# Two value units of a decode attention kernel, each loaded by two queues

## The chip, the core and the metric

The kernel runs on one core of one Trainium2 chip. The engines that matter here are TensorE (PE), VectorE (DVE), ScalarE (ACT) and SyncE (SP). SyncE and ScalarE can both issue loads from the chip's memory into the on-chip memory of 128 partitions; each has a queue of its own in the profile (q1 is SyncE's, q10 ScalarE's), and the packets of both are moved by the core's 16 DMA engines. The metric is the device time of one execution in microseconds, as the median of the runs.

## The reference

One token is decoded against a long cache. `x` has 448 values; there are 16 query heads in 8 groups of two that share a key and value head, 65536 cached positions and a head size of 256. Everything large is bf16. Cut to what matters:

```python
xn = layernorm(x)
q = (xn @ wq).reshape(1, 1, 16, 256)              # 16 query heads
scores = einsum(q, k_cache) * 256 ** -0.5         # k_cache: 8 x 65536 x 256, each head for two queries
o = softmax(scores) @ v_cache                     # v_cache: 8 x 65536 x 256
attn = o.reshape(1, 1, 4096) @ wo                 # 4096 x 448
r = xn @ w_r                                      # a router over one token: it is always chosen
y = (silu(xn @ w_gate) * (xn @ w_up)) @ w_down * sigmoid(r)
out = x + attn + xn + y
```

The two caches are 512 MB (2 x 8 x 65536 x 256 x 2 bytes); wq, wo and the three feed-forward matrices are some 12 MB more. Each byte is used once.

## The kernel before

**Units and slots.** Each head's 65536 positions are spread over the 128 partitions, 512 consecutive positions in each. The kernel cuts a head into four units of 128 positions in each partition. A unit is thus 128 stretches of 64 KB, one to a partition, 8 MB in all. Keys make 32 units and values 32. The tensor `ring` holds three slots of one unit each: slots 0 and 1 take keys, slot 2 takes values. A slot is a semaphore too (`slot0` to `slot2`): a load adds 16 to it when it is complete, and PE waits for the count that the unit it needs will bring it to.

**Order of loads.** The list of loads is written out by hand and issued by SyncE in that order: `item` puts the waits that a load needs, and then the load, on SyncE's program. The waits are on PE having done with what stood in the slot: `FREE, u` is the end of PE's transposes of key unit u, `VFREE, t` the end of its products with value unit t. Keys run one head ahead of values, so that the softmax's maximum of a head is known when its values are used.

**The end.** The last head's values are the units NT to NT + 3 (28 to 31). There are no keys left by then, so the key slots take values too. SyncE's list ends like this, where `slot_item(kind, unit, slot, parts, waits)` loads one unit:

```python
slot_item("v", NT, 0, None, [("FREE", NU - 2)])
item("wg", ...); item("wd", ...); item("wo", ...)     # into slot 2, after VFREE NT - 1
slot_item("v", NT + 1, 1, None, [("FREE", NU - 1)])
slot_item("v", NT + 2, 0, None, [("VFREE", NT)])
slot_item("v", NT + 3, 1, ...two parts..., [("VFREE", NT + 1)])
# then the last rows of wo, in five small loads
```

"The second and third units" of the change are NT + 1 and NT + 2. NT + 3 goes into the slot of NT + 1, so it is issued only when PE has used NT + 1.

On PE, `ending` puts its work in this order: the maximum of the last head, `values(NT)`, the feed-forward (`pe_ffn1`, `pe_ffn_hT`, `pe_ffn2`), the output product of the first seven heads (`pe_attn`), `values(NT + 1)`, `values(NT + 2)`, `values(NT + 3)`, and the output product of the last head. `values(t)` is 64 matmuls into `ps_o`, in two chunks (`pe_V`), each after ScalarE has copied the softmax weights of its positions (`p_sb`, by `act_pc`).

ScalarE has two small loads of its own there: `hop` writes the outputs of the first seven heads to memory (`o_flat`) and reads them back in another layout (`oT_h`). All loads of the program show as one line of the source in the profile, L892.

Of the kernel before, what the change touches and what calls it, by code (L numbers as in the profile page):

```python
# [21 lines left out]
def bass_parallel_sum__gqa_block_cached__moe_arch_mod__decode_kernel(  # L22
# [20 lines left out]
    P = 128  # L43
    _, Hkv, Sk, Dh = A_k_cache.shape
# [16 lines left out]
    SBN = HC * CH  # L61
    SETS = SBN // SETN
    U = NPP // SBN
    NT = U * (Hkv - 1)
    NU = U * Hkv
# [27 lines left out]
    slots = [ring[:, i * SLOT:(i + 1) * SLOT] for i in range(NSLOT)]  # L93
# [98 lines left out]
    prog = {e: [] for e in engines}  # L192
    here = [("S", 0)]
# [7 lines left out]
    def put(e, kind, key, fn, sem):  # L201
        if ghost[0] and e == "pe":
            prog[e].append(("g" + kind, lab(e), key, fn, sem))
        elif not ghost[0]:
            prog[e].append((kind, lab(e), key, fn, sem))

    def W(e, *key):
        put(e, "w", key, None, None)
# [3 lines left out]
    def O(e, key, fn, sem=None, n=1):  # L212
        key = key if isinstance(key, tuple) else (key,)
        if not ghost[0]:
            weight[key] = n
        put(e, "o", key, fn, sem or e)
# [17 lines left out]
    items = {}  # L234
    semtot = {}
    fed = {}

    def item(key, parts, need=()):
        for n in need:
            W("sp", *n)  # L240
        for ap, src, sem in parts:
            semtot[sem] = semtot.get(sem, 0) + 16
            items[key] = (sem, semtot[sem])
            prog["sp"].append(("d", here[0], ("DMA", key, len(prog["sp"])), (ap, src), sem))

    def rows_src(kd, u, o, J):
        src = A_k_cache if kd == "k" else A_v_cache
        n0 = (u % U) * SBN + o
        return src[0, u // U].rearrange("(p n) d -> p n d", p=P)[:, n0:n0 + J, :]

    def slot_item(kd, u, s, parts=None, need=()):

        o = 0
        for k, (sem, J) in enumerate(parts or [("slot%d" % s, SBN)]):
            ap = slots[s][:, o * Dh:(o + J) * Dh]
            item((kd, u, k), [(ap.rearrange("p (j d) -> p j d", d=Dh), rows_src(kd, u, o, J), sem)],
                 need[k] if isinstance(need, dict) else need if k == 0 else ())
            o += J
        fed[(kd, u)] = (s, parts or [("slot%d" % s, SBN)])

    def flat_src(src, n):
        return src.rearrange("a b -> (a b)").rearrange("(p n) -> p n", p=P)

# [6 lines left out]
    def wo_rows(f0, f1):  # L270

        return A_wo[0:(Hq - rep) * Dh, :].rearrange("(p f) n -> p f n", f=FR)[:, f0:f1, :].rearrange("p f n -> p (f n)")
# [21 lines left out]
    item("wg", [(wg_area[:, 0:WGN // 2], flat_src(B_w_gate, F), "wg"), (wg_area[:, WGN // 2:WGN], flat_src(B_w_up, F), "wg")], [("VFREE", NT - 1)])  # L294
    item("wd", [(wd_area.rearrange("p (s x) -> p s x", s=2), B_w_down.rearrange("(s p t) n -> p s (t n)", s=2, p=P), "wd"), (x_again, A_x[0], "wd")])
    item("wo", [(wo_all[:, 0:(FR - WX) * D], wo_rows(0, FR - WX), "wo")])
    slot_item("v", NT + 1, 1, None, [("FREE", NU - 1)])
    slot_item("v", NT + 2, 0, None, [("VFREE", NT)])
    slot_item("v", NT + 3, 1, [("last%d" % k, J) for k, J in enumerate(LAST)], [("VFREE", NT + 1)])
    LATE_AT = [FR - sum(LATE[k:]) for k in range(len(LATE) + 1)]  # L300
    for k in range(len(LATE)):
# [107 lines left out]
    def mm(*a, **k):  # L409
        return pe.matmul(*a, **k)  # L410
# [87 lines left out]
    def k_JT(s):  # L498
        u, sl = divmod(s, SETS)
        W("pe", "EVQ", s)  # L500
        if sl == 0:
            W("pe", "SCOPY", u - 1)
        n0 = sl * SETN

        def f(it):
            for jj in range(GN):
                o = ps_sn[:, n0:n0 + SETN, :].rearrange("p (m j) i -> p m j i", j=GN)[:, :, jj, :]
                ins = mm(o, lhsT=s2[s % 2][:, jj * P:(jj + 1) * P], rhs=sel_bf[:, :, :], start=True, stop=True)
            return ins

        O("pe", ("JT", s), f, "jt")
        if sl == SETS - 1:
            dve_scopy(u)
# [14 lines left out]
    def pe_m1t(b):  # L528
        W("pe", "M1", b)
        W("pe", "OTSB", min(b - U, NT - 1))  # L530
        O("pe", ("M1T", b), lambda it: mm(ps_m[0:rep, C_BIG:C_BIG + P], lhsT=m1[:, :], rhs=ident_f[:, :],
                                          is_transpose=True, start=True, stop=True))
        W("dve", "M1T", b)
        O("dve", ("GMAX", b), lambda it: nc.vector.tensor_reduce(out=gmax[:, :], in_=ps_m[0:rep, C_BIG:C_BIG + P], axis=AX.X, op=ALU.max))
        W("dve", "GMAX", b)
        W("dve", "BC", b - 1)
        O("dve", ("DIAG", b), lambda it: nc.vector.tensor_scalar(out=diag[:, :], in0=ident_f[0:rep, 0:rep], scalar1=gmax[:, 0:1],  # L537
                                                                 scalar2=None, op0=ALU.mult))
# [25 lines left out]
    def pe_tot(t):  # L564
        W("pe", "NEGMAX", t + U - 1)
        W("pe", "PC", t, 0)

        def f(it):
            return mm(ps_m[0:P, C_TOT:C_TOT + NH * rep].rearrange("p (f i) -> p f i", f=NH), lhsT=ones_f[:, :],
                      rhs=rowsum[:, :].unsqueeze(1).to_broadcast([P, NH, rep]), start=True, stop=True)  # L570

        O("pe", ("TOT", t), f)
        W("dve", "TOT", t)
        W("dve", "OTSB", t - 1)
        O("dve", ("RS", t), lambda it: nc.vector.reciprocal(out=rs[:, :, :], in_=ps_m[0:P, C_TOT:C_TOT + NH * rep]))  # L575
# [81 lines left out]
    def hop(k, dst, src):  # L657
        items["oh", k] = ("oh%d" % k, 16)
        prog["act"].append(("d", here[0], ("DMA", "oh", k), (dst, src), "oh%d" % k))
# [116 lines left out]
    def values(t):  # L776
        for c in range(HC):
            pe_V(t, c, t == NT, t == NU - 1, True)

    def ending():  # L780
        here[0] = ("S", 1)
        T = NU - 1
        n = NU * SETS
        k_JT(n - 2)
        k_QK(n - 1)
        pe_turn()
        k_JT(n - 1)
        W("pe", "OROW")
        pe_m1t(T)
        pe_bc(T)  # L790
        W("pe", "OTSB", NT - 1)
        W("act", "DMA", ("oh", 0))
        hop(1, oT_h[:, :], o_flat.rearrange("r d -> (r d)").rearrange("(p f) -> p f", f=FR))
        values(NT)
        pe_tot(NT)
        pe_ffn1()
        pe_ffn_hT()
        pe_ffn2()
        pe_attn()
        W_item("dve", "wd")  # L800
        O("dve", "XN_AGAIN", lambda it: nc.vector.tensor_scalar(out=xn_again, in0=x_again, scalar1=stat[0:1, 7:8], scalar2=stat[0:1, 4:5],
                                                                op0=ALU.add, op1=ALU.mult))
        W("dve", "XN_AGAIN")
        W("dve", "FFN2")
        W("dve", "ATTN")
        W("dve", "SIG")
        O("dve", "YS", lambda it: nc.vector.scalar_tensor_tensor(
            out=sum_f, in0=ps_y, scalar=stat[0:1, 6:7], in1=xn_again, op0=ALU.mult, op1=ALU.add))
        W("dve", "YS")
        O("dve", "YX", lambda it: nc.vector.tensor_tensor(out=sum_f, in0=sum_f, in1=x_again, op=ALU.add))  # L810
        W("dve", "YX")
        O("dve", "SUM", lambda it: nc.vector.tensor_tensor(out=sum_f, in0=ps_a, in1=sum_f, op=ALU.add))
        values(NT + 1)
        W("pe", "SUM")
        W("pe", "SCOPY", T)

        O("pe", "FIN_BASE", lambda it: fin(sum_f, 0, ones_f[0:1, 0:1], first=True))
        values(NT + 2)
        values(NT + 3)
        dve_ob(T)  # L820
        pe_oT(T)

        def fin_x(it, k):
            for f in range(*LATE_AT[k:k + 2]):
                ins = fin(wo_all, f * D, oT_h[:, f:f + 1])
            return ins

        for k in range(len(LATE)):
            W_item("pe", ("wx", k))
            O("pe", ("FIN_X", k), lambda it, k=k: fin_x(it, k))  # L830
        W("pe", "OTSB", T)
        for k, (i, f0, f1) in enumerate(ENDS):
            W_item("pe", ("wo_end", k))

            def f(it, k=k, i=i, f0=f0, f1=f1):
                for hf in range(f0, f1):
                    ins = fin(wo_end, (i * NH + hf) * D, oT_sb[:, hf, i:i + 1], last=k == len(ENDS) - 1 and hf == f1 - 1)
                return ins

            O("pe", ("FIN", k), f)  # L840
        W("dve", "FIN", len(ENDS) - 1)
        W("act", "FIN", len(ENDS) - 1)
        O("act", ("RESULT", 1), lambda it: nc.scalar.activation(out=res_bf[:, DA:D], in_=ps_s[32:33, 0:D - DA], func=ACTF.Copy), "res")  # L843
        O("dve", ("RESULT", 0), lambda it: nc.vector.tensor_copy(out=res_bf[:, 0:DA], in_=ps_s[0:1, 0:DA]), "res")
        W("sp", "RESULT", 0)
        W("sp", "RESULT", 1)
        prog["sp"].append(("d", here[0], ("OUT", 0), (out[0], res_bf), "out"))
# [275 lines left out]
```

## Time and profile before

| what | value |
|---|---|
| median of 3 runs | 1275.57 us (1275.52 to 1275.57) |
| the profiled execution | 1275.83 us |
| its span, from the first to the last instruction | 1274.5 us |
| granted TensorE clock, mean | 0.889 |
| PE busy | 953.0 us, 75% |
| DVE busy | 570.5 us, 45% |
| ACT busy | 436.9 us, 34% |
| moved by DMA | 549.22 MB, 431 GB/s over the span |

Times in the profile are microseconds from the start of the span. A row of a timeline gives the start, the duration, the engine (a q behind its name is the engine's queue of instructions that issue DMAs), the source line, the operation, what is written and read, the count, and in brackets how long the engine sat idle before it and what ended that. PE's busy share is high because its matmuls fill the time between loads; whether it or the loads set the pace is read from what its idle time waits for. The landing time of a load is counted from its issue, so it includes the time that it stands in its queue behind earlier loads.

### The profile page before, as it was taken

Reading aid. Unit: us, or ns where it says so; the run is one execution under the profiler, and the core shown is the slowest. Engines: PE = TensorE matmul, PEld = TensorE weight load, DVE = VectorE, ACT = ScalarE, POOL = GpSimd, SP = SyncE. Lnnn points to the kernel's source line nnn. Section 1 sums busy time; section 2 is a strip of 40 time slices with the busy share of each in tenths; the row PEclk is TensorE's granted clock in tenths of the full one; section 3 lists DMA queues with packets and bytes.
Section 4 is the critical chain, followed back from the end, with each engine's and each line's share of the span. In section 5 each row is a group of like instructions: output and inputs, shape, how many; then the busy total and the mean of one; then the engine's idle time right before and its main releaser. Section 6 shows DMA issues by size and latency. Waiting matters only on the chain. (4 is left out here: it accounts for less than half of the span.)

```text
span 1274.5 us, 23469 instructions
## 1 busy us (share of the span) xinstructions
PE 953.0 (75%) x9718; PEld 625.3 (49%) x9718; DVE 570.5 (45%) x1078; ACT 436.9 (34%) x656; POOL 8.0 (1%) x38
## 2 busy tenths in 40 slices
PE   3998977678767769777778677687777688777844
PEld 3676655445544445444455454454454555444411
DVE  4665544445434455444454344453444544444310
ACT  1554533244322433324233243343333334323300
POOL 2000000000000000000000000000000000000000
PEclk9998998889888899888899888898878988888876
DMA  9999999999999999999999999999999999999998
GB/s 406 430 434 431 443 430 430 438 428 442 432 432 428 438 430 442 430 432 432 434 430 442 430 432 436 430 436 436 432 430 438 428 436 436 432 430 438 426 431 367
DMA packets 11841, 549.22 MB, mean 431 GB/s; under 512 B 1442, under 2 KB 1844, under 8 KB 2356
## 3 DMA queue, kind: packets, MB, share of 16 engines
q1 hardware_dynamic: 11652, 549.03, 99.7%
q8 instruction: 8, 0.13, 0.0%
q10 hardware_dynamic: 176, 0.02, 0.0%
q14 instruction: 5, 0.04, 0.0%
HBM read 549.04 MB, written 0.01 MB: 431 GB/s over the span
## 5 line engine op out<-in xcount | busy, mean ns | idle before, releaser
L410 PE MATMUL ps_t<-ident_f,ring 128*128 128x128 f32 x4096 | 589.2, 286 | 83.6 <-DMA ring<-in_A_k_cache_dram 62.7
L469 DVE COPY kt_all<-ps_t 128x1024 bf16<-128x1024 bf16 x768 | 487.0, 685 | 295.6 <-PE ps_q L410 291.3
L410 PEld LDWEIGHTS ps_t<-ident_f,ring 128*128 128x128 f32 x4096 | 452.7, 144 | 236.3 <-issue 134.6
L471 ACT ACTIVATE kt_all<-ps_t 128x1024 bf16<-128x1024 bf16 x256 | 262.2, 1024 | 501.7 <-PE ps_q L410 501.6
L410 PE MATMUL ps_o<-ring,p_sb 128*4 128x512 bf16 x2048 | 177.1, 508 | 213.8 <-DMA ring<-in_A_v_cache_dram 208.9
L410 PEld LDWEIGHTS ps_o<-ring,p_sb 128*4 128x4 bf16 x2048 | 53.8, 102 | 302.6 <-issue 277.9
L410 PE MATMUL ps_q<-kt_all,q_cur 128*2 128x512 bf16 x2056 | 164.7, 397 | 0.3 <-DVE kt_all L469 0.3
L493 ACT ACTIVATE s<-ps_q 98x512 bf16<-98x512 f32 x257 | 151.8, 591 | 1.3 <-PE ps_q L410 1.3
L575 DVE RECIPROCAL rs<-ps_m 128x4 f32<-128x4 f32 x29 | 5.3, 183 | 271.5 <-PE ps_m L410 271.5
L562 ACT ACTIVATE p_sb<-S_sb 128x128 bf16<-128x128 bf16 x64 | 18.9, 307 | 271.4 <-PE ps_o L410 271.2
L410 PEld LDWEIGHTS ps_s<-sel_bf,s 128*128 128x128 bf16 x1032 | 64.1, 97 | 4.5 <-ACT s L493 1.3
L613 DVE CAST ob_sb<-ps_o 100x512 bf16<-100x512 f32 x29 | 20.1, 692 | 99.0 <-PE ps_o L410 99.0
L410 PE MATMUL ps_s<-sel_bf,s 128*128 128x8 bf16 x1032 | 63.3, 167 | 1.0 <-ACT s L493 1.0
L410 PEld LDWEIGHTS ps_q<-kt_all,q_cur 128*2 128x2 bf16 x2056 | 26.4, 79 | 45.2 <-issue 45.2
L410 PEld LDWEIGHTS ps_m<-rowsum,ones_f 128*128 128x128 f32 x58 | 11.8, 255 | 21.3 <-issue 21.3
L471 ACT ACT_TABLE_LOAD x7 | 9.0, 1283 | 27.8 <-PE ps_q L410 27.8
L522 DVE TENSOR_REDUCE m1p<-S_sb (+1 forms) x33 | 13.9, 422 | 4.4
L410 PE MATMUL ps_m<-rowsum,ones_f 128*128 128x4 f32 x58 | 14.4, 318 | 0.0
L552 ACT ACTIVATE S_sb<-S_sb,negmax 128x512 bf16<-128x512 bf16 x16 | 13.2, 851 | 3.3 <-DVE negmax L546 3.3
L410 PE MATMUL ps_m<-diag,ones_f 2*128 2x2 f32 x58 | 11.2, 260 | 3.8 <-DVE diag L537 1.0
L410 PEld LDWEIGHTS ps_m<-diag,ones_f 2*128 2x128 f32 x58 | 8.7, 187 | 10.7 <-DVE diag L537 10.7
L520 DVE CAST S_sb<-ps_s 128x256 f32 (+1 forms) x33 | 13.7, 416 | 0.1
(90 smaller groups left out, 122.7 us busy)
## 6 DMA issues: line engine op xcount, KB each, us to landing
ring<-in_A_k_cache_dram SPq DMA_DIRECT2D x10, 4096.0 KB, 28.4
ring<-in_A_v_cache_dram SPq DMA_DIRECT2D x1, 6144.0 KB, 27.3
ring<-in_A_wq_dram SPq DMA_DIRECT2D x1, 3584.0 KB, 11.2
ring<-in_A_v_cache_dram SPq DMA_DIRECT2D x1, 2048.0 KB, 31.9
ring<-in_A_wo_dram SPq DMA_DIRECT2D x1, 1792.0 KB, 26.8
ring<-in_B_w_gate_dram SPq DMA_DIRECT2D x1, 1568.0 KB, 16.3
ring<-in_B_w_up_dram SPq DMA_DIRECT2D x1, 1568.0 KB, 19.6
ring<-in_B_w_down_dram SPq DMA_DIRECT2D x1, 1568.0 KB
```

Of the source, the lines that this page charges most:

```text
L410: return pe.matmul(*a, **k)
L469: O(e, ("EV", s, m), lambda it: nc.vector.tensor_copy(out=kt[:, :], in_=tb[:, :]), f"ev{m}")
L471: O(e, ("EV", s, m), lambda it: nc.scalar.activation(out=kt[:, :], in_=tb[:, :], func=ACTF.Copy), f"ev{m}")
L493: O("act", ("EVQ", s), lambda it: nc.scalar.activation(out=s2[s % 2][0:QROWS, :], in_=ps_q[0:QROWS, :], func=ACTF.Copy), "evq")
L520: O("dve", ("SCOPY", u), lambda it: nc.vector.tensor_copy(out=S_sb[:, at(it, SBN), :], in_=ps_sn), "sc")
L522: O("dve", ("SMAX", u), lambda it: nc.vector.tensor_reduce(out=m1p[:, :, at(it, 1)], in_=S_sb[:, at(it, SBN), :].rearrange("p n i -> p i n ...
L552: O("act", ("EXP", h, i), lambda it, i=i: nc.scalar.activation(out=S_sb[:, :, i], in_=S_sb[:, :, i], func=ACTF.Exp, bias=negmax[:, i:i + 1 ...
L562: O("act", ("PC", t, c), lambda it: nc.scalar.activation(out=p_sb[:, c, :, :], in_=S_sb[:, n:n + CH, :], func=ACTF.Copy), "pc")
L575: O("dve", ("RS", t), lambda it: nc.vector.reciprocal(out=rs[:, :, :], in_=ps_m[0:P, C_TOT:C_TOT + NH * rep]))
L613: O("dve", ("OB", t), lambda it: nc.vector.tensor_copy(out=ob_sb[0:OROWS, :], in_=ps_o[0:OROWS, :]))
```

## The change

Units NT + 1 and NT + 2 are each loaded in two halves by partition. SyncE issues partitions 0 to 63 at the place where it issued the whole unit, after the same waits. ScalarE issues partitions 64 to 127, after the same waits put on its own program: for NT + 1 directly behind the second `hop`, for NT + 2 behind the program part `values(NT)`. Both halves add 16 to the slot's semaphore, and PE waits for the sum. No unit, slot or wait of PE changes besides.

```diff
+    def shared_item(u, s, need):
+        ap = slots[s].rearrange("p (j d) -> p j d", d=Dh)
+        src = rows_src("v", u, 0, SBN)
+        sem = "slot%d" % s
+        item(("v", u, 0), [(ap[0:P // 2], src[0:P // 2], sem)], need)
+        other[u] = (ap[P // 2:P], src[P // 2:P], sem, need)
+        semtot[sem] += 16
+        items[("v", u, 0)] = (sem, semtot[sem])
+        fed[("v", u)] = (s, [(sem, SBN)])
+
+    def ask_other(u):
+        ap, src, sem, need = other[u]
+        for n in need:
+            W("act", *n)
+        prog["act"].append(("d", here[0], ("DMA", "other", u), (ap, src), sem))
...
-    slot_item("v", NT + 1, 1, None, [("FREE", NU - 1)])
-    slot_item("v", NT + 2, 0, None, [("VFREE", NT)])
+    shared_item(NT + 1, 1, [("FREE", NU - 1)])
+    shared_item(NT + 2, 0, [("VFREE", NT)])
...
         hop(1, oT_h[:, :], o_flat.rearrange("r d -> (r d)").rearrange("(p f) -> p f", f=FR))
+        ask_other(NT + 1)
         values(NT)
+        ask_other(NT + 2)
         pe_tot(NT)
```

On ScalarE's program the place is the end, from the write of `o_flat` to the sigmoid of the feed-forward (the two activations that write `kt_all` from `ps_t`). Before:

```order
L892 DMA o_flat<-kt_all 14x256
L552 ACTIVATE S_sb,rowsum<-S_sb,negmax 128x512 x2
L562 ACTIVATE p_sb<-S_sb 128x128 x2
L892 DMA oT_h<-o_flat 128x28
L562 ACTIVATE p_sb<-S_sb 128x128 x2
L688 ACT_TABLE_LOAD
L688 ACTIVATE kt_all<-ps_t 2x448 x2
```

And after, where the lines of the source are 19 to 21 higher:

```order
L913 DMA o_flat<-kt_all 14x256
L571 ACTIVATE S_sb,rowsum<-S_sb,negmax 128x512 x2
L581 ACTIVATE p_sb<-S_sb 128x128 x2
L913 DMA oT_h<-o_flat 128x28
L913 DMA ring<-in_A_v_cache_dram 64x32768
L581 ACTIVATE p_sb<-S_sb 128x128 x2
L913 DMA ring<-in_A_v_cache_dram 64x32768
L707 ACT_TABLE_LOAD
L707 ACTIVATE kt_all<-ps_t 2x448 x2
```

The two loads of `ring` from 64 partitions' worth of values are new: one between the hop and the weights of the next unit, one ahead of the table load.

On SyncE's program the place is the last six loads of `ring`. Before:

```order
L892 DMA ring<-in_A_x_dram 1x448
L892 DMA ring<-in_A_wo_dram 128x7168
L892 DMA ring<-in_A_v_cache_dram 128x32768 x2
L892 DMA ring<-in_A_v_cache_dram 128x24576
L892 DMA ring<-in_A_v_cache_dram 128x8192
```

And after:

```order
L913 DMA ring<-in_A_x_dram 1x448
L913 DMA ring<-in_A_wo_dram 128x7168
L913 DMA ring<-in_A_v_cache_dram 64x32768 x2
L913 DMA ring<-in_A_v_cache_dram 128x24576
L913 DMA ring<-in_A_v_cache_dram 128x8192
```

The two whole units have become two halves at the same places; what stands before and behind them is as it was.

More of the change, by code (lines that the diff above doesn't have):

```diff
@@ L259, in slot_item @@
         fed[(kd, u)] = (s, parts or [("slot%d" % s, SBN)])
+    other = {}
+    def shared_item(u, s, need):
[12 more added lines that the diff above has]
+        prog["act"].append(("d", here[0], ("DMA", "other", u), (ap, src), sem))
     def flat_src(src, n):
```

## The prediction

> **What bounds the kernel now.** I read the queue table of the page first, to see whether the loads are the limit at all.
>
> ```profile
> DMA packets 11841, 549.22 MB, mean 431 GB/s; under 512 B 1442, under 2 KB 1844, under 8 KB 2356
> q1 hardware_dynamic: 11652, 549.03, 99.7%
> q10 hardware_dynamic: 176, 0.02, 0.0%
> ```
>
> The reader is to see that one queue, q1 (SyncE's), moves all but 0.02 MB, and that its packets fill 99.7% of the 16 engines' time. q10 is ScalarE's. The kernel is a stream of 549 MB at one pace; it gets shorter only if the pace rises or a hole closes, and there is next to no hole.
>
> Second, the tail on the engine that uses the data: PE's timeline from 1218 us, where "idle before" names what it waited for.
>
> ```profile
> 1218.28 3.19 PE L410 MATMUL ps_q<-ring,oT_h 128*1 128x448 bf16 x16
> 1229.45 6.36 PE L410 MATMUL ps_o<-ring,p_sb 128*4 128x512 bf16 x64 [7.99 <-DMA ring<-in_A_v_cache_dram]
> 1248.82 5.22 PE L410 MATMUL ps_o<-ring,p_sb 128*4 128x512 bf16 x64 [12.51 <-DMA ring<-in_A_v_cache_dram]
> 1263.34 3.58 PE L410 MATMUL ps_o<-ring,p_sb 128*4 128x512 bf16 x32 [9.31 <-DMA ring<-in_A_v_cache_dram]
> 1267.41 2.74 PE L410 MATMUL ps_o<-ring,p_sb 128*4 128x512 bf16 x32 [0.48 <-PEq L1077]
> ```
>
> The four starts are the landings of units NT+1, NT+2 and the two parts of NT+3. Each wait ends with a load. The step from 1229.45 to 1248.82 is the pace: 19.37 us for one unit of 8.39 MB, which is 433 GB/s. A unit is 128 packets of 64 KB, eight for each engine, so one packet takes 19.37 / 8 = 2.42 us.
>
> Third, SyncE's queue: when each load is issued.
>
> ```profile
> 1183.18 0.34 SPq L892 DMA_DIRECT2D ring<-in_A_wo_dram  x1
> 1192.67 0.33 SPq L892 DMA_DIRECT2D ring<-in_A_v_cache_dram  x1
> 1206.05 0.33 SPq L892 DMA_DIRECT2D ring<-in_A_v_cache_dram  x1
> 1235.86 0.80 SPq L892 DMA_DIRECT2D ring<-in_A_v_cache_dram  x2
> ```
>
> NT+1 is issued 36.8 us before it lands and NT+2 42.8 us. NT+3 is issued at 1235.86, 12.96 us before NT+2 has landed. The queue never runs dry here, so a second issuer closes no gap.
>
> **The change part by part.** *Issues and waits.* ScalarE gets two more issues. Its timeline around them, before:
>
> ```profile
> 1200.16 0.51 ACT L562 ACTIVATE p_sb<-S_sb 128x128 bf16<-128x128 bf16 x2
> 1200.47 0.36 ACTq L892 DMA_DIRECT2D oT_h<-o_flat  x1
> 1204.16 0.31 ACT L562 ACTIVATE p_sb<-S_sb 128x128 bf16<-128x128 bf16 x1 [3.49 <-PE ps_o L410]
> 1206.05 0.31 ACT L562 ACTIVATE p_sb<-S_sb 128x128 bf16<-128x128 bf16 x1 [1.58 <-PE ps_o L410]
> 1206.38 1.28 ACT L688 ACT_TABLE_LOAD   x1
> 1209.09 0.96 ACT L688 ACTIVATE kt_all<-ps_t 2x448 f32<-2x448 f32 x2 [1.42 <-PE ps_t L410]
> ```
>
> The first issue comes behind the hop at 1200.47 + 0.36 = 1200.83. Its wait, FREE of the last key unit, was over when SyncE issued at 1192.67. It costs 0.36 us inside 3.49 us of idle time: zero. The second comes behind the copy of 1206.05. Its wait, VFREE of NT, is what that copy had just waited for: zero. It pushes the table load by about 0.36 us, to an end at 1208.0, and the activation behind it could not start before 1209.09: zero. Without that cover the sigmoid and the feed-forward would be 0.36 us later, which PE's 7.99 us of idle time before NT+1 takes up. SyncE issues as many loads as before, with the same waits. PE waits for the same semaphore, at a count that both halves make up; the price of that is only the later of the two halves.
>
> *When ScalarE's half can flow.* It stands in q10 behind the hop of oT_h:
>
> ```profile
> ring<-in_A_wo_dram SPq DMA_DIRECT2D x1, 1792.0 KB, 26.8
> oT_h<-o_flat ACTq DMA_DIRECT2D x1, 7.0 KB, 12.0
> ```
>
> These 7 KB need 12.0 us, though at the stream's pace they are worth 0.02 us: packets of q10 take turns with packets of q1 on each engine. The hop is through at 1200.47 + 12.0 = 1212.5, and wo, the last load ahead of NT+1 in q1, at 1183.18 + 26.8 = 1210.0. So both halves of NT+1 begin at about the same time, and neither the feed-forward's weights nor wo are pushed back by more than a packet or two. From then on each engine takes turns between a packet for the lower partitions and one for the upper, four of each for a unit, through NT+1 and NT+2: 16 packets, 38.7 us at the old pace.
>
> [...]
>
> *What a half costs.* No row of this trace has a sizeable transfer to fewer than 128 partitions, so the price has two ends. Lower end: the engines are the limit, and the pace stays at 2.42 us a packet, +0. A gain isn't in reach, since the engines' time is already 99.7% full. Upper end: the pace belongs to the ways into the partitions. Then 128 partitions take 16 packets at 2.42 us at a time, 64 take only eight, and 16 engines that all write the same half need 4.84 us a packet: +38.7 us over two units. [...] The phases of the engines are in a window of 5 us, 40 slices of 0.125 us, in which 524 is the start of one 64 KB packet:
>
> ```profile
> GB/s 0 0 0 524 0 0 0 0 1573 524 1049 0 0 524 524 1049 1573 524 524 0 0 0 0 524 0 0 0 1049 1049 1049 0 0 0 524 1049 1049 1049 1049 0 0
> DMA packets 32, 2.10 MB, mean 419 GB/s; under 512 B 0, under 2 KB 0, under 8 KB 0
> ```
>
> 32 starts are two rounds of 16. In the first round there are 1 and 6 starts up to the eleventh slice and 9 from the 14th to the 19th; the second starts with the 24th. [...] I take +28.7. I prefer the upper side to zero because the pace is one number in every stage (431 GB/s over the span, 433 here), and what the edit changes is exactly which partitions 16 engines write at once.
>
> *What follows it.* NT+1 lands about 14 us later, at 1244; PE needs 6.36 us, so NT+3 is issued near 1250. NT+2 lands at 1248.82 + 28.7 = 1277.5, so the queue still has 27 us in hand and no hole opens. NT+3 and the rest of wo go to 128 partitions as before, and the chain at the end keeps its lengths:
>
> ```profile
> 1267.41 2.77 PE ps_o L410 x32
> 1270.21 0.70 DVE ob_sb L613
> 1271.21 1.75 PE ps_s L410 x31
> 1272.98 0.36 ACT kt_all L843
> ```
>
> Sum: issues 0, waits 0, halves +28.7, tail 0. The profiled execution took 1275.83 us (span 1274.5 and 1.33 around it), 0.26 above the median of the runs. 1275.83 + 28.7 - 0.26 = 1304.3, so 1304.
>
> **The rivals.** *The halves interleave without loss.* If the engines are the limit, or an engine keeps both halves in flight so that both sides of the memory are always written, the total bytes and the pace are unchanged: NT+2 lands at 1248.8 again and the time is 1275.6. For it: every engine has one packet of each half in turn, so over two packets both halves are used evenly. [...]
>
> [...]
> [...]
>
> *A hole before NT+3.* If ScalarE's half were first served in turn with the weights, NT+1 would be complete only after everything issued before NT+2's lower half. That is 4.2 MB or 9.7 us later, at 1239; with PE's 6.36 us NT+3 is issued at 1245.5, and NT+2, ending at 1248.8 at full pace, leaves 3.3 us for the start of a transfer. If a start takes more, the stream stands still for the rest. The hop's 12.0 us include waiting, so they bound the start: a hole of at most 8.7 us, 1284, more likely 1278. Against it: the hop ahead in q10.
>
> **How the numbers follow.** Sharing with lags (+15 to +37 us): 0.46. Lockstep (over +37): 0.14. A hole, or a small loss of 3 to 15 us: 0.09. No loss: 0.27. Some gain that no row explains: 0.04. About 0.2% (2.6 us) is what a measurement of this kernel can tell from no change. So slower is 0.46 + 0.14 + 0.09 = 0.69, same 0.27, faster 0.04. The likeliest case gives 1304, its own range 1291 to 1313. The range that leaves out no more than 2 in 10 must take in the no-loss case: 1275 to 1313.
>
> **What the profile of the changed kernel would show.** q10 carries about 8.4 MB and packets of 64 KB. ScalarE's two issues stand near 1201 and 1206.4. If I am right, PE's start on NT+1 moves from 1229.45 to about 1244 and on NT+2 from 1248.82 to about 1277, NT+3 follows NT+2 by the same 14.5 us, and the DMA row stays at a full share while GB/s falls to some 250 (433 / 1.74) in between. If there is no loss, GB/s stays near 430 throughout, and the starts stay. A hole would show as a low DMA share after NT+2. [...]

## The result, and the profile after

| | before | after |
|---|---|---|
| median, us | 1275.57 (4 runs, 1275.52 to 1275.77) | 1320.14 (4 runs, 1313.7 to 1324.95) |
| ratio to before | 1 | 1.0336, 95% interval 1.0292 to 1.038 |
| profiled execution, us | 1275.83 | 1313.7 |
| its span, us | 1274.5 | 1312.4 |

The change costs 44.6 us by the medians. The profiled execution is the fastest of the four and shows 37.9 of them; the experiments come back to the rest.

The queue table of the page after:

```profile
DMA packets 11873, 549.22 MB, mean 418 GB/s; under 512 B 1474, under 2 KB 1876, under 8 KB 2388
q1 hardware_dynamic: 11524, 540.65, 96.9%
q10 hardware_dynamic: 336, 8.40, 2.8%
```

The bytes are the same, 8.4 MB of them have moved to ScalarE's queue, and the engines are as busy as they were: 96.9 and 2.8 make 99.7%. A full queue doesn't mean a full pace. That is in the windows (the last number of a row is GB/s, the one ahead of it the engines' busy share). After, from where the halves begin:

```profile
1210.00:1230.00 20.00, 6.67 (x30) 2.57 (x28) 2.37 (x6) 0.02 (x1) 0.00 (x0) 0.70 1.01 223
1230.00:1250.00 20.00, 5.37 (x16) 1.76 (x16) 1.90 (x3) 0.00 (x0) 0.00 (x0) 0.59 1.01 239
1250.00:1270.00 20.00, 3.37 (x35) 1.12 (x38) 0.00 (x0) 0.00 (x0) 0.00 (x0) 0.50 0.98 220
```

And before, in the same places:

```profile
1210.00:1230.00 20.00, 10.26 (x54) 4.17 (x56) 4.29 (x9) 0.04 (x1) 0.00 (x0) 0.78 0.98 426
1230.00:1250.00 20.00, 7.49 (x80) 2.27 (x72) 0.00 (x0) 0.62 (x2) 0.00 (x0) 0.59 1.00 432
```

With a busy share of 1.0 in both, the stream moves 220 to 239 GB/s in place of 426 to 432. PE's timeline after shows what that does to the landings:

```profile
1230.53 5.37 PE L429 MATMUL ps_q<-ring,oT_h 128*1 128x448 bf16 x16 [12.11 <-DMA ring<-in_A_wo_dram]
1266.63 6.52 PE L429 MATMUL ps_o<-ring,p_sb 128*4 128x512 bf16 x64 [30.73 <-DMA ring<-in_A_v_cache_dram]
1287.16 6.49 PE L429 MATMUL ps_o<-ring,p_sb 128*4 128x512 bf16 x64 [13.52 <-DMA ring<-in_A_v_cache_dram]
1301.34 3.58 PE L429 MATMUL ps_o<-ring,p_sb 128*4 128x512 bf16 x32 [7.69 <-DMA ring<-in_A_v_cache_dram]
1305.41 2.49 PE L429 MATMUL ps_o<-ring,p_sb 128*4 128x512 bf16 x32 [0.49 <-PEq L1098]
```

NT+1 lands at 1266.6 (before 1229.5), NT+2 at 1287.2 (1248.8), and NT+3 follows NT+2 by 14.2 us (14.5). So the 38 us of this execution arise in the two halved units and nowhere behind them. Nearly all of them, 37.2, are there when NT+1 lands. By the packets of the trace, 192 of the 256 packets of the two units have ended by then (before: 136), though NT+1 has only 128: 64 packets of NT+2's halves had ended before the last of NT+1's. NT+3 waits for PE to have used NT+1, so it is issued late too, at 1273.19 in place of 1235.86:

```profile
1273.19 5.17 SPq L913 DMA_DIRECT2D ring<-in_A_v_cache_dram  x2
```

PE also waits 12.11 us for wo, which has landed 47.2 us after its issue, not 26.8:

```profile
ring<-in_A_wo_dram SPq DMA_DIRECT2D x1, 1792.0 KB, 47.2
ring<-in_A_v_cache_dram ACTq DMA_DIRECT2D x2, 73.4
```

wo isn't on the path: PE would have waited for NT+1 anyway.

### The profile page after: what moved, and what is told of

It is laid out like the page before. It is cut to its first block, busy times and chain, and to the rows that moved or that the text cites. A ratio compares the mean times of both kernels' runs of the same rounds, so it can differ in the third digit from the quotient of the medians.

```text
span 1312.4 us, 23471 instructions
## 1 busy us (share of the span) xinstructions
PE 963.4 (73%) x9718; PEld 628.3 (48%) x9718; DVE 570.6 (43%) x1078; ACT 436.5 (33%) x656; POOL 8.0 (1%) x38
## 3 DMA queue, kind: packets, MB, share of 16 engines
q1 hardware_dynamic: 11524, 540.65, 96.9%
## 5 line engine op out<-in xcount | busy, mean ns | idle before, releaser
L429 PE MATMUL ps_o<-ring,p_sb 128*4 128x512 bf16 x2048 | 184.2, 524 | 234.5 <-DMA ring<-in_A_v_cache_dram 229.7
L632 DVE CAST ob_sb<-ps_o 100x512 bf16<-100x512 f32 x29 | 20.1, 691 | 126.3 <-PE ps_o L429 126.3
L429 PE MATMUL ps_q<-ring,oT_h 128*1 128x448 bf16 x16 | 5.4, 517 | 12.1 <-DMA ring<-in_A_wo_dram 12.1
## 6 DMA issues: line engine op xcount, KB each, us to landing
ring<-in_A_wo_dram SPq DMA_DIRECT2D x1, 1792.0 KB, 47.2
```

Of the source, the lines that this page charges most:

```text
L632: O("dve", ("OB", t), lambda it: nc.vector.tensor_copy(out=ob_sb[0:OROWS, :], in_=ps_o[0:OROWS, :]))
```

## The experiments

Two questions were open after the result: what makes the halves slow, and why two halves beside each other don't make up for it. e3 to e8, e10 and e11 are one execution each; the kernel before spread over 0.9 us in its largest set of runs beside them (15 runs, 1275.52 to 1276.39). Where only some of the partitions are loaded (e3, e5, e7, e8), values are left out and the kernel computes something else; only its time counts there.

### Is it the halves, the two queues, or the reading?

**e1_one_queue.** Both halves by SyncE, one behind the other. The lines are against the kernel before, shown in part: `halves_item` loads the ranges of partitions that are listed at its end, each as a load of its own.

```diff
-    slot_item("v", NT + 1, 1, None, [("FREE", NU - 1)])
-    slot_item("v", NT + 2, 0, None, [("VFREE", NT)])
+    halves_item(NT + 1, 1, [("FREE", NU - 1)], [(0, P // 2), (P // 2, P)])
+    halves_item(NT + 2, 0, [("VFREE", NT)], [(0, P // 2), (P // 2, P)])
```

> NT+1 and NT+2 are each loaded as two halves by partition again, but both halves by SyncE, the lower first, the upper directly behind it. Theory 1, the way into 64 partitions is half as wide as that into 128: a half takes 19.4 us in place of 9.7, whoever issues it, so +38.7 us, 1314, and some less where the end of one half overlaps the start of the next (1305 to 1314). Theory 2, taking turns between two queues with 64 KB packets halves the pace: one queue only, so 1275.6. Theory 3, the memory is slow to read 64 rows that lie 256 KB apart: as theory 1.

Measured: 1320.09 us (4 runs, 1319.5 to 1321.0), ratio 1.0348 (1.0331 to 1.0365). One queue is as slow as two, so theory 2 falls here. It's 6 us over theory 1's upper end. PE's timeline shows a part of the reason:

```profile
1252.55 6.24 PE L418 MATMUL ps_o<-ring,p_sb 128*4 128x512 bf16 x64 [31.80 <-DMA ring<-in_A_v_cache_dram]
1292.77 4.92 PE L418 MATMUL ps_o<-ring,p_sb 128*4 128x512 bf16 x64 [33.48 <-DMA ring<-in_A_v_cache_dram]
```

From NT+1 to NT+2 it is 40.2 us. A half takes 20.1 us, not the 19.4 that an exact doubling gives. Over four halves that is some 3 of the 5.4 us by which e1's loss of 44.1 is above 38.7; the rest is there when NT+1 lands, and the runs don't say from what.

**e2_positions.** Two queues, but split by position, so that each load goes to all 128 partitions.

```diff
-        item(("v", u, 0), [(ap[0:P // 2], src[0:P // 2], sem)], need)
-        other[u] = (ap[P // 2:P], src[P // 2:P], sem, need)
+        item(("v", u, 0), [(ap[:, 0:CH], src[:, 0:CH], sem)], need)
+        other[u] = (ap[:, CH:SBN], src[:, CH:SBN], sem, need)
```

> Two queues as in the change, but each unit is split by position: SyncE loads the first 64 positions of all 128 partitions, ScalarE the other 64. Theory 1 (the way into 64 partitions): all partitions are written all the time, so 1275.6 within 0.2%. Theory 2 (taking turns between queues): as slow as the change, 1310 to 1325. Theory 3 (reading 64 rows): 1275.6.

Measured: 1276.02 us (10 runs), ratio 1.0 (0.9991 to 1.001), and the pace is full:

```profile
1210.00:1230.00 20.00, 9.15 (x43) 3.67 (x41) 3.73 (x8) 0.00 (x0) 0.00 (x0) 0.76 1.01 434
1230.00:1250.00 20.00, 6.34 (x68) 1.99 (x68) 0.00 (x0) 0.62 (x2) 0.00 (x0) 0.59 1.02 438
```

The same two queues, the same places in both programs and the same bytes cost nothing when each load covers all partitions. The packets are of 32 KB here, not 64; e9 below has two queues with packets of 64 KB. With it theory 2 falls altogether.

**e3_lower_only.** The halves alone, one queue, nothing beside them.

```diff
+    halves_item(NT + 1, 1, [("FREE", NU - 1)], [(0, P // 2)])
+    halves_item(NT + 2, 0, [("VFREE", NT)], [(0, P // 2)])
```

> Of NT+1 and NT+2 only partitions 0 to 63 are loaded, by SyncE; the upper partitions keep what stood in the slot, so 8.4 MB of values are left out. Theory 1 (the way into 64 partitions is half as wide): 4.2 MB take as long as 8.4 MB did, 19.4 us, so NT+1 and NT+2 land at 1229 and 1249 as before and the time is 1275.6 with 8.4 MB less. Theory 2 (two queues): full pace on one queue, 9.7 us a unit, so about 19 us less, 1256 to 1259. Theory 3 (reading): as theory 1.

Measured: 1279.85 us, one run beside 1275.99 of before. With 8.4 MB less to load the kernel is 4 us slower. Two windows of 10 us, and the packets of the 20 us from 1215:

```profile
1212.00:1222.00 10.00, 6.34 (x37) 2.91 (x37) 2.97 (x7) 0.00 (x0) 0.00 (x0) 1.00 1.02 210
1222.00:1232.00 10.00, 0.00 (x0) 0.00 (x0) 0.00 (x0) 0.00 (x0) 0.00 (x0) 0.50 0.98 203
DMA packets 80, 4.19 MB, mean 210 GB/s; under 512 B 16, under 2 KB 16, under 8 KB 16
```

80 packets of which 16 are tiny leave 64 of 64 KB in 20 us, four for each engine: some 5 us for each, where the whole unit has 2.42. The landings are 1232.78 and 1253.15, 20.4 us for 4.2 MB. This is the price by itself: half the bytes take 5% longer than the whole.

**e4_near_rows.** The change, with the source rows of a unit next to each other.

```diff
-        src = rows_src("v", u, 0, SBN)
+        r0 = (u - NT) * P * SBN
+        src = A_v_cache[0, Hkv - 1][r0:r0 + P * SBN].rearrange("(p n) d -> p n d", p=P)
```

> The change, but NT+1 and NT+2 read a contiguous 8 MB of the last head's values, a 64 KB stretch next to the other for each partition, in place of stretches 256 KB apart; the values are thus other positions' than the softmax weights'. Theories 1 and 2: as slow as the change, 1310 to 1325. Theory 3 (the memory is slow to read 64 rows 256 KB apart): back to 1275.6, or much of the way.

Measured: 1316.63 us, one run, inside the spread of the change's runs:

```profile
1210.00:1230.00 20.00, 5.45 (x24) 1.97 (x22) 1.60 (x4) 0.00 (x0) 0.00 (x0) 0.65 1.02 225
1250.00:1270.00 20.00, 0.92 (x12) 0.39 (x16) 0.00 (x0) 0.00 (x0) 0.00 (x0) 0.51 0.97 233
```

Rows next to each other bring no pace back, so theory 3 falls. What is left is which partitions are written.

### Which sets of partitions are slow?

The next runs set three pictures against each other, all of them guesses. A: engines collide only where they write the same small block of partitions, and the others keep their pace. B: as soon as some collide, all are slowed. C: there are just two sides, the lower and the upper 64 partitions.

**e5_sixteen.** Only partitions 0 to 15 are loaded; the edit is e3's with `[(0, 16)]`.

> Of NT+1 and NT+2 only partitions 0 to 15 are loaded, by SyncE, 1 MB each; the other partitions keep what stood there, so 14.7 MB of values are left out. [...] C, just two sides, lower and upper 64 partitions: 5.1 us a unit, 14 us from issue to landing. [...]

Measured: 1261.0 us, and from issue to landing:

```profile
ring<-in_A_v_cache_dram SPq DMA_DIRECT2D x1, 24.4
1212.00:1217.00 5.00, 4.04 (x26) 2.07 (x27) 0.92 (x3) 0.00 (x0) 0.00 (x0) 1.00 1.08 118
1217.00:1222.00 5.00, 2.30 (x13) 0.84 (x10) 1.89 (x3) 0.00 (x0) 0.00 (x0) 0.98 0.71 92
```

24.4 us, not C's 14: 16 neighbouring partitions get only about a quarter of the pace, 92 to 118 GB/s in place of 433. The limit is finer than two sides.

**e7_even.** 64 partitions again, but every second one: `ap[0:P:2]`.

> Of NT+1 and NT+2 only the even partitions are loaded, by SyncE, 64 of 128 and spread over both sides; the odd ones keep what stood there, so 8.4 MB of values are left out. A and B, engines that write the same block of partitions at the same moment collide, wherever the blocks lie: about as the lower half alone, 1276 to 1281. C, two sides, lower and upper: no collision, full pace, 1256 to 1260.

Measured: 1256.28 us, 19.2 us below before.

```profile
1210.00:1215.00 5.00, 3.25 (x18) 1.30 (x16) 1.60 (x4) 0.00 (x0) 0.00 (x0) 0.80 1.00 433
1215.00:1220.00 5.00, 5.00 (x30) 2.13 (x29) 0.00 (x0) 0.00 (x0) 0.00 (x0) 0.86 0.97 419
```

419 to 433 GB/s: the full pace with 64 partitions. The number of partitions is thus not what counts, and my A and B, which expected a collision here, are wrong. C gave the right number here and the wrong one in e5. What the runs leave is this: the load of every second partition ran at the full pace (419 to 433 GB/s); those of neighbours were slower, 64 of 128 at a half (203 to 210, e3) and 16 at about a quarter (92 to 118), not an eighth.

**e8_ninetysix.** Partitions 0 to 95: `[(0, 96)]`.

> Of NT+1 and NT+2 only partitions 0 to 95 are loaded, by SyncE, six packets for each engine; the rest keep what stood there, so 4.2 MB of values are left out. A, only engines that write the same block collide and the others run at full pace: packets of 2.4 and of 5.1 us side by side, GB/s between 210 and 430. B, as soon as some collide all engines are slowed: all packets near 5.1 us, 205 to 225 GB/s, 31 us a unit, about 1298. C, two sides: the lower 64 at the slow pace and the upper 32 as well, all near 5 us.

Measured: 1301.34 us.

```profile
1212.00:1232.00 20.00, 8.02 (x37) 3.32 (x37) 3.12 (x7) 0.00 (x0) 0.00 (x0) 0.73 1.00 213
1232.00:1252.00 20.00, 6.69 (x68) 2.10 (x68) 0.00 (x0) 0.62 (x2) 0.00 (x0) 0.59 0.97 204
```

204 to 213 GB/s, no more than for 64. That is what B expected, and C too, but not A: no 64 KB packet of the trace from 1212 to 1262 is near 2.42 us, nearly all take 4.6 to 5.1. Three quarters of the partitions don't give three quarters of the pace. None of the three pictures fits all of e5, e7 and e8, so what makes one set of partitions slower than another stays open.

**e9_even_odd.** The change's two queues, with the even partitions on SyncE's and the odd ones on ScalarE's.

```diff
-        item(("v", u, 0), [(ap[0:P // 2], src[0:P // 2], sem)], need)
-        other[u] = (ap[P // 2:P], src[P // 2:P], sem, need)
+        item(("v", u, 0), [(ap[0:P:2], src[0:P:2], sem)], need)
+        other[u] = (ap[1:P:2], src[1:P:2], sem, need)
```

> The change with the halves cut the other way: SyncE loads the even partitions of NT+1 and NT+2, ScalarE the odd ones. Theory 1 in its first form (any 64 partitions are half as wide a way): as slow as the change, 1310 to 1325. Theory 1 as the single even half left it (only which blocks of partitions are written at the same moment counts, and every second partition over all 128 covers all of them): 1275.6 within 0.2%, with two queues and two halves. If two queues with halves by partition cost something of themselves: 1279 or more.

Measured: 1275.83 us (11 runs), ratio 1.0001 (0.9992 to 1.001), and

```profile
1210.00:1230.00 20.00, 5.29 (x31) 2.22 (x29) 2.04 (x5) 0.00 (x0) 0.00 (x0) 0.71 1.00 431
1230.00:1250.00 20.00, 10.66 (x99) 3.73 (x101) 1.89 (x3) 0.62 (x2) 0.00 (x0) 0.84 0.99 426
ring<-in_A_wo_dram SPq DMA_DIRECT2D x1, 1792.0 KB, 47.4
```

Two halves by partition on two queues, with 64 KB packets, at full pace: the whole cost of the change is in the choice of which 64. It also separates the delay of wo from the rest. wo lands as late as in the change (47.4 us): 92 of its 128 packets of 14 KB start after ScalarE's first 64 KB packet and take turns with those, and that costs nothing. The split gains nothing either: no version here that loads everything beats the kernel before, whose stream was already full.

### Why don't the two halves overlap?

**e6_one_unit.** The change for NT+1 only; NT+2 whole, by SyncE.

> The change for NT+1 alone; NT+2 is loaded whole by SyncE. If the cost belongs to each half unit, half of the change's: +19 to +22 us, 1295 to 1298. If the start of the alternation (weights beside halves) is what costs, nearly all of it: over 1305.

Measured: 1302.77 us, 27 us over before; more than half of the change and less than "nearly all".

```profile
1210.00:1230.00 20.00, 4.86 (x30) 2.08 (x27) 2.25 (x6) 0.00 (x0) 0.00 (x0) 0.72 1.00 203
1256.40 5.23 PE L429 MATMUL ps_o<-ring,p_sb 128*4 128x512 bf16 x64 [15.77 <-DMA ring<-in_A_v_cache_dram]
1275.85 5.74 PE L429 MATMUL ps_o<-ring,p_sb 128*4 128x512 bf16 x64 [13.72 <-DMA ring<-in_A_v_cache_dram]
```

PE starts on NT+1 at 1256.40 and on NT+2 19.45 us later, so the whole unit runs at its old pace and all 27 us lie ahead of it. The pace is as low as that of a half alone, but the two halves were hardly side by side here. By the packets of the trace, the upper half starts at 1204.9, when 91 of wo's 128 packets have yet to start, and 54 of its 64 packets have started before the first of the lower half, at 1225.0. So wo ran beside the upper half, and it was slowed as well: each of its 51 packets from 1206 to 1225.0 took 1.04 to 1.30 us in place of 0.54, although wo goes to all 128 partitions. NT+1 and the 1.3 MB of wo that were left, 9.7 MB at 205 GB/s in place of 433, make some +25 us, an estimate; that is most of the 27.

**e10_shifted.** One tiny load more on ScalarE's queue, ahead of its half (shown in part; the end of the program also waits for it).

```diff
+        prog["act"].append(("d", here[0], ("SHIFT", 0), (spare[0:8, 0:8], A_v_cache[0, 0, 0:8, 0:8]), "shift"))
         ask_other(NT + 1)
```

> The change, with one more load ahead of ScalarE's first half on its queue: 8 rows of 16 bytes into a tensor that nothing reads. [...] If all engines are slowed as soon as halves are in flight, whatever their order: as the change, 1310 to 1325.

Measured: 1317.67 us, and

```profile
1210.00:1230.00 20.00, 9.92 (x37) 3.57 (x36) 1.60 (x4) 0.00 (x0) 0.00 (x0) 0.67 0.98 218
1230.00:1250.00 20.00, 1.36 (x6) 0.42 (x4) 1.89 (x3) 0.00 (x0) 0.00 (x0) 0.59 1.01 223
```

No relief. The load was meant to set some engines behind the others, in case the halves are slow only because the engines are in step. That isn't settled: the profile doesn't name the engine of a packet, so it's not shown which engines the load moved, if any.

**e11_again.** The change once more.

> The change once more, with a profile, for the spread of its runs (1313.7 to 1325.0). If the spread comes from how the two queues' packets interleave, wo, NT+1 and NT+2 land at other times than in the first profile while the packets are as slow; if it comes from holes in the stream, the DMA share drops somewhere after NT+1.

Measured: 1317.16 us, 3.5 above the first profile. wo lands after 49.0 us and NT+1 at 1269.7, 3.1 us later than in the first profile, so nearly all of the difference is there when NT+1 lands. The share of the engines seems to drop behind it:

```profile
1250.00:1270.00 20.00, 0.27 (x4) 0.13 (x8) 0.00 (x0) 0.00 (x0) 0.00 (x0) 0.50 1.05 233
1270.00:1280.00 10.00, 5.22 (x68) 1.65 (x60) 0.00 (x0) 0.62 (x2) 0.00 (x0) 0.84 0.85 205
1280.00:1290.00 10.00, 0.00 (x0) 0.00 (x0) 0.00 (x0) 0.00 (x0) 0.00 (x0) 0.50 0.88 247
```

But that is no hole. A row counts the whole time of a packet where the packet begins, and these take near 4.7 us; the row ahead reads 1.05. By the starts and durations of the packets in the trace, at least 16 are under way at every moment from 1200 to 1305, in this profile and in the first one. That leaves, of the two expected causes, the way in which the two queues' packets interleave. Whether it also makes the slower runs, up to 1325, is not shown; there is no profile of one.

## Why the prediction was wrong

It forecast 1304, with 1275 to 1313 as the range; the median is 1320. Point by point:

- *The stream bounds the kernel, and a second issuer closes no gap.* Right: e2 and e9 use the second issuer without any effect (ratios 1.0 and 1.0001).
- *Issues and waits cost nothing.* Right. ScalarE issued at 1200.8 and 1206.0, the activation behind the table load started at 1209.06 (before 1209.09).
- *Which partitions are written sets the price.* Right, and shown against two rivals, the queues and the reading, by e2, e4 and e9. But the prediction's picture of a lower and an upper half is too simple: 16 neighbours are slower still than 64 (92 to 118 against 203 to 210 GB/s), and 96 no faster (204 to 213).
- *The upper end, "16 engines that all write the same half need 4.84 us a packet", +38.7.* Mis-sized by 5.4 us: a half alone takes 20.4 us in e3 and 20.1 in e1, not 19.37, and e1, in which the halves don't run side by side, lost 44.1.
- *"Halves +28.7" in the sum.* This is the step that failed. It supposed that the two halves, side by side, give back 10 of the 38.7 us; no run shows that term, nor the 1.74 of the forecast "some 250 (433 / 1.74)". The runs show packets slow while halves are in flight, also those of loads to all partitions. In e6 every packet of wo from 1206 to 1225.0 is slow (1.04 to 1.30 us in place of 0.54). In e3 the 48 KB packets of NT+3, a load to all partitions, that start before the half's last packet ends take 1.93 to 3.96 us, all 20 of them; those behind take 1.82. In e8 no 64 KB packet keeps its 2.42; nearly all take 4.6 to 5.1. By the medians the second half beside the first gives back nothing: 1320.1 with two queues and 1320.1 with one half behind the other. In single profiles it gives back a little: 220 to 239 GB/s against 203 to 210 for a half alone, and 1313.7 and 1317.2 us against 1319.5 of e1's. So the sum had +28.7 where e1 shows 28.7 + 10.0 (no relief) + 5.4 (the upper end) = 44.1, and the change itself 44.6. Why all these packets slow down together is not shown: the profile names neither the engine nor the partition of a packet.
- *Lockstep (over +37), chance 0.14.* The case that came true: +37.9 in the profile and +44.6 by the medians, so two halves as slow as one after the other (+44.1 in e1). Its cause is not shown; the slow packets above, and e10 without relief, speak against engines that are merely in step. Beside the first half, the second gained 5 to 18% of pace in the first profile (220 to 239 against 203 to 210 GB/s), and nothing by the medians. This holds for halves of neighbours only: the even and the odd half, also two loads, reach the full pace together (426 to 431 GB/s in e9).
- *"Neither the feed-forward's weights nor wo are pushed back by more than a packet or two."* Wrong for wo, by 20.4 us (47.2 against 26.8). By the trace, ScalarE's first 64 KB packet starts at 1207.3, 5 us before the 1212.5 of the prediction, with 19 of wo's 128 packets still to start; those take turns with packets of 64 KB. It cost nothing, as e9 shows. That packets of q10 take turns with packets of q1 is in the trace of before: from 1204.6 to 1206.6, while the hop's packets go, 59 packets of q10 begin and 60 of q1. That each engine does so by itself is not shown, since no packet names its engine.
- *NT+1 at 1244, "27 us in hand", "no hole opens".* No hole opened: at least 16 packets are under way throughout in both profiles of the change. But the margin was half of what was forecast. NT+1 landed 37 us late, not 14, so NT+3 was issued at 1273.2, 14.0 us before NT+2 landed.

## What to carry to other kernels

Ask of each load which partitions it reaches, not only how large it is: here the same 4.2 MB ran at 419 to 433 GB/s into every second partition and at 203 to 210 into the lower 64, and the busy share of the DMA engines read 0.97 to 1.02 in both. A second queue was worth nothing to a stream that was already full (ratios 1.0 and 1.0001 in e2 and e9), and beside its large packets the small ones of wo landed 20.4 us later. If a load has to be split, try it by position (e2) or by every second partition (e9), which cost nothing here, and not into neighbouring halves, which cost 44.6 us.

## What the runs showed of the hardware that I had not expected

- 64 partitions can be at full pace (even ones, 419 to 433 GB/s), at half (0 to 63, 203 to 210), and 96 are no faster than 64 neighbours (204 to 213); 16 neighbours reach 92 to 118.
- The price of a half is a little more than a doubling: alone it moved 206 GB/s (4.19 MB in 20.37 us), 5% below half of 433.
- A load that is in flight beside a half is slowed with it, though it goes to all partitions: wo's packets in e6 took 1.04 to 1.30 us in place of 0.54.
- With the slow halves on two queues the time varied more: the changed kernel's four runs spread over 11 us, those with the same halves on one queue over 1.5 us, and two queues at full pace over 0.5 us (e2, 10 runs) and 1.1 us (e9, 11 runs).
